# The first expert's weights: asked for later, laid out by column pieces, split one by one

## The chip, the cores and the metric

One core of one Trainium2 chip runs the whole program. The metric is device time in microseconds for one execution: the median of the runs of a kernel.

## The reference

Attention with a local window and block summaries is followed by a mixture-of-experts layer that sends every token to one expert. Cut to what matters:

```python
# q, k, v: [4 batches, 8 heads, 768 positions, 64]
scores = concat(mask(|i-j| < 16, q k^T / 8), q max32(k)^T / 8 + log 32)
x = softmax(scores) @ concat(v, mean32(v))          # -> [4, 768, 512], float32
logits = x @ w_gate                                  # [4, 768, 8 experts]
for b, s:                                            # a chain along s
    e = argmax(logits) if s == 0 or sigmoid(x @ w_local) < 0.5 else previous e
    h = max(x[b, s] @ w1[e], 0)                      # w1[e]: 512 x 1024
    out[b, s] = softmax(logits)[e] * (h @ w2[e])     # w2[e]: 1024 x 512
```

## The kernel before

**Attention.** 16 pairs of heads (4 batches, 4 pairs each) are worked through in 32 groups, two groups per pair. The main loop runs over G = 0 to 34, because it is a pipeline: iteration G makes the scores of group G (`s_mm`, L309 and L315), the maxima on VectorE (L321) and the exponentials on ScalarE (L325), transposes group G-2 (`t_stage`, L335, copied by ScalarE at L336), multiplies group G-3 with v (`a_mm`, L346) and normalises it into a tile `xs` (`a_norm`, L361 and L362). `a_mm` has one PSUM bank, which comes free when L362 has read it. There are three `xs` tiles for the eight that are written, and each is stored to `x_dram` by SyncE (L452, 876 KB) before it is written again. SyncE's queue also issues all loads, in program order; the last load of attention is `load_w(15)` (L182) in iteration 28.

**Beside attention.** When batch 0 is done, its routing (`route(0)`, then `early()`) runs on VectorE in small steps between the steps of attention. It finds the expert `e0` that takes most tokens of batch 0, and the rows of six blocks of 128 tokens, of which the first two are gathered from `x_dram`. `TIME` and `MORE` say how many of these small steps fit in each gap of an iteration, from iteration 28 on by the third entry of `TIME`.

**The first expert's weights.** w1 and w2 of `e0` come as eight chunks of 128 x 1024 float32 (512 KB): 0 to 3 are w1, 4 to 7 are w2. A chunk is fetched into one of four buffers `wst` (`wfetch`, L977, on SyncE) and then split into a high and a low part (`wsplit`): ScalarE copies the high part (L981), and the low part is a subtraction, on VectorE in one instruction (L984) or on GpSimd in four pieces of 256 columns (L989). `WBY` names the engine of each chunk. Chunk j of w1 holds the rows k = j of all 1024 columns. `WFETCH` and `WSPLIT` give the iterations in which chunks are fetched and chunks 0 to 3 split; a fetch of chunk 4 to 7 waits until the split of chunk 0 to 3 has left its buffer.

**The expert layer.** Blocks of 128 rows are worked through in pairs (`pair`). `tx` transposes a block of 128 gathered rows and splits it (L999, L1001). Layer 1 goes over four pieces of 256 columns of w1, each of two halves j with four k and three products (L1104 to L1106): 16 steps of six matmuls, and at the end of each piece ScalarE's ReLU (L1110) and VectorE's low part (L1112). Layer 2 (L1023 to L1025) takes eight slices of w2, twice. `START` puts the two `tx` and step 0 of layer 1 into iterations 33 and 34. After iteration 34, `last()` issues the other steps, splits w2's chunks after the steps given by `WLAST`, and between steps lets `flow` issue routing steps of batches 1 to 3 (`route(1)`, then `finish`), which run mostly on VectorE with a few small TensorE operations (L563 is the first). All engines work in program order.

Of the kernel before, what the change touches and what calls it, by code (L numbers as in the profile page):

```python
# [19 lines left out]
P = 128  # L20
# [11 lines left out]
E, DM, DF = 8, 512, 1024  # L32
KT, FT = DM // P, DF // P
# [13 lines left out]
OOB = 4096  # L47
WARM = 44

WFETCH = (25, 26, 26, 27, 28, 29, 30, 31)  # L50
WSPLIT = (28, 29, 30, 31)
WBY = "VGGVVGVG"

WLAST = (2, 5, 8, 11)
START = ((33, 1), (34, 0), (34, 1))
FIRST_L1 = 16

SPLIT_BY = ("VGVV", "VGVG")
# [2 lines left out]
PW1, PW2 = (0, 2, 4, 6), (10, 12, 14, 15)  # L61

ON_PE = {"PE": 2, "PE late": 4, "ACT": 4}
TIME, MORE = ((0.5, 0.2, 0.3), (0.7, 0.4, 0.3), (0.9, 0.5, 0.4)), 28

C_T, C_PE, C_WAIT, C_LONG, C_DVE, C_LAT, AHEAD = 0.65, 0.8, 0.3, 1.3, 0.14, 0.05, 1.5

# [3 lines left out]
class Kernel:  # L71
# [945 lines left out]
        self.split_ps(ps, h, l)  # L1017
        return h, l

    def mm(self, ps, ah, al, w, c0, first, last):  # L1020
        nc = self.nc
        wh, wl = self.hi[w][:, c0:c0 + 512], self.lo[w][:, c0:c0 + 512]
        nc.tensor.matmul(out=ps, lhsT=ah, rhs=wh, start=first, stop=False)  # L1023
        nc.tensor.matmul(out=ps, lhsT=ah, rhs=wl, start=False, stop=False)  # L1024
        nc.tensor.matmul(out=ps, lhsT=al, rhs=wh, start=False, stop=last)  # L1025
# [36 lines left out]
    def few(self, j):  # L1062

        nc, fw, b = self.nc, self.fw, j
        s1, s2 = self.raw
        ps = self.bank("s")[:, 0:DF // 4]
        for k in range(KT):
            for q in range(4):
                c0 = k * DF + DF // 4 * q
                nc.tensor.matmul(out=ps[FEW * q:FEW * q + FEW], lhsT=self.xf[b][:, k], rhs=s1[:, c0:c0 + DF // 4],  # L1070
                                 start=(k == 0), stop=(k == KT - 1))
        h = fw.tile([P, DF // 4], F32, name="fh")
        nc.scalar.activation(out=h, in_=ps, func=AF.Relu)
        yield
        ps = self.bank("t")[:, 0:DF // 4]
        for c in range(2):
            nc.tensor.transpose(out=ps[:, P * c:P * c + P], in_=h[:, P * c:P * c + P], identity=self.ident)
        hT = fw.tile([P, 2, 4, FEW], F32, name="fhT")
        nc.vector.tensor_copy(out=hT.rearrange("p c q t -> p (c q t)"), in_=ps)
        yield  # L1080
        ps = self.bank("a")[:, 0:P]
        for f in range(FT):
            for q in range(4):
                c0 = f * DM + P * q
                nc.tensor.matmul(out=ps[FEW * q:FEW * q + FEW], lhsT=hT[:, f % 2, f // 2], rhs=s2[:, c0:c0 + P],
                                 start=(f == 0), stop=(f == FT - 1))
        y = fw.tile([P, P], F32, name="fy")
        nc.vector.tensor_scalar(out=y, in0=ps, scalar1=self.p4[b], scalar2=None, op0=ALU.mult)
        nc.gpsimd.indirect_dma_start(out=self.out.rearrange("t (q d) -> (t q) d", q=4),
                                     out_offset=bass.IndirectOffsetOnAxis(ap=self.idx4[b], axis=0),  # L1090
                                     in_=y, in_offset=None, bounds_check=4 * T_ALL - 1, oob_is_err=False)

    def pair(self, i, mid, w1, w2):

        nc = self.nc
        xT, hT = self.xT, self.hT
        for f in range(0, FT, 2):
            ps = self.bank("s").rearrange("p (f t) -> p f t", f=2)
            for j in range(2):
                for k in range(KT):  # L1100
                    c0 = k * DF + P * (f + j)
                    xh, xl = [xT[:, k, part].rearrange("p h t -> p (h t)") for part in range(2)]
                    wh, wl = [w[0][:, c0:c0 + P] for w in (self.hi, self.lo)]
                    nc.tensor.matmul(out=ps[:, j], lhsT=wh, rhs=xh, start=(k == 0), stop=False)  # L1104
                    nc.tensor.matmul(out=ps[:, j], lhsT=wh, rhs=xl, start=False, stop=False)  # L1105
                    nc.tensor.matmul(out=ps[:, j], lhsT=wl, rhs=xh, start=False, stop=(k == KT - 1))  # L1106
                    if k % 2:
                        yield
            h, l = hT[:, f:f + 2, 0], hT[:, f:f + 2, 1]
            nc.scalar.activation(out=h, in_=ps, func=AF.Relu)  # L1110
            self.dve(0.6, self.t + 0.5)
            nc.vector.scalar_tensor_tensor(out=l, in0=ps, scalar=0.0, in1=h.bitcast(F32), op0=ALU.max, op1=ALU.subtract)  # L1112
        for half in range(2):
            yp = self.bank("a")
            s = slice(P * half, P * half + P)
            for f in range(FT):
                self.mm(yp, hT[:, f, 0, s], hT[:, f, 1, s], 1, f * DM, f == 0, f == FT - 1)
                yield
                j = FT * half + f
                pm = PM if i else PM0  # L1120
                if j in pm:
                    mid(pm.index(j))
                for at, w in (PW1, w1), (PW2, w2):
                    if j in at:
                        w(*(q for q in range(4) if at[q] == j))
            self.store(yp, 2 * i + half, 2 * i < EARLY)
        yield

    def single(self, i, mid, w1, w2):

        nc, fw = self.nc, self.fw
        hs = [fw.tile([P, 512], F32, name=f"hs{f}") for f in range(2)]

        def mm1(f, ks):
            for k in ks:
                if k == 0:
                    self.hp = self.bank("s")
                self.mm(self.hp, self.xT[:, k, 0, 0], self.xT[:, k, 1, 0], 0, k * DF + 512 * f, k == 0, k == KT - 1)
                if k == KT - 1:
                    nc.scalar.activation(out=hs[f], in_=self.hp, func=AF.Relu)  # L1140

        mm1(0, range(KT))
        mm1(1, (0, 1))
        hT = [self.th(hs[0], "h0"), None]
        mm1(1, (2, 3))
        w1(0, 1)
        yp = self.bank("a")

        def mm2(ks):
            for k in ks:  # L1150
                h, l = [x[:, P * (k % 4):P * (k % 4) + P] for x in hT[k // 4]]
                self.mm(yp, h, l, 1, k * DM, k == 0, k == FT - 1)

        mm2((0, 1))
        hT[1] = self.th(hs[1], "h1")
        mm2((2, 3))
        for h in range(2):
            mid(h)
        w1(2, 3)
        mm2(range(4, 8))  # L1160
        self.store(yp, i)
        w2(0, 1, 2, 3)

    def run(self):
        nc, tc = self.nc, self.tc
        CH = 1024
        NCH = KT * DF // CH
        jobs, st = {}, {}

        def at(G, point, f, *args):  # L1170
            jobs.setdefault((G, point), []).append((f, args))

        def wfetch(j):
            w, q = divmod(j, NCH)
            st["w", j] = self.awk.tile([P, CH], F32, name="wst", bufs=4)
            self.fetch(st["w", j], w, q * CH, (q + 1) * CH, st["e0"])

        def wsplit(j):
            w, q = divmod(j, NCH)
            self.split(w, q * CH, (q + 1) * CH, st.pop(("w", j)), nc.vector if WBY[j] == "V" else nc.gpsimd)  # L1180

        def have_e0():
            st["e0"] = nc.values_load(self.e0[0:1, 0:1], engines=(ENG.SP,), min_val=0, max_val=E - 1)
            for j in range(2 * NCH):
                if j < NCH:
                    at(WSPLIT[j], 1, wsplit, j)
                at(WFETCH[j], 1, wfetch, j)

        def have_rows(s0, s1):
            st["told"] = s1  # L1190
# [3 lines left out]
        def ask_rows():  # L1194
            st["rows"] = s1 = st["told"]
            while st["next"] < min(s1, st["free"]):
                self.gather(st["next"])
                st["next"] += 1
# [10 lines left out]
        def block0():  # L1209
            self.mw2 = self.pool("m_wk2")  # L1210
            self.xT = self.mw2.tile([P, KT, 2, 2, P], F32R, name="xT")
            self.hT = self.mw2.tile([P, FT, 2, 2 * P], F32R, name="hT")
            for i in range(2):
                while st["next"] <= i:
                    self.small(1, True)
                    ask_rows()
                self.tx(i, i)
                freed()
                yield

        def last():
            st["attention"] = False
            ask_rows()
            self.later(self.wait(), self.route(NS - 1), self.finish())
            for k in range(FIRST_L1):
                next(first)
                if k in WLAST:
                    wsplit(NCH + WLAST.index(k))
                self.flow(C_T)

        def reg(i, engines, hi):
# [54 lines left out]
        first = chain(block0(), self.pair(0, *calls(2)))  # L1286

        for G, i in START:
            at(G, i, lambda: next(first))
# [168 lines left out]
```

## Time and profile before

| | us |
|---|---|
| median of 3 runs | 444.74 (443.76 to 449.13) |
| the profiled execution, its own time | 444.76 |
| its span in the trace | 443.0 |
| TensorE busy in the span | 409.0 (92%) |
| mean granted TensorE clock | 0.987 of full speed |

The trace is one execution. Its times run from the start of the span, and 1.76 us of the execution's own time lie outside it. In the rows below, a time in square brackets is what the engine sat idle before an instruction, with what ended the wait. A name that ends in q (SPq) is an engine's sequencer.

### The profile page before, as it was taken

How to read it: one execution, taken by the hardware profiler on the slowest of the kernel's cores; microseconds unless marked ns; L12 is line 12 of the kernel's file. 1: busy time of each engine (PE TensorE's matmuls, PEld its weight loads, DVE VectorE, ACT ScalarE, POOL GpSimd, SP SyncE). 2: the span in 40 equal slices, each digit the busy share in tenths (PEclk: the TensorE clock that was granted, in tenths of full speed). 3: DMA queues.
4: the chain of work that ended last, by engine and by line, in shares of the span. 5: the costliest groups of instructions: out<-in, count | busy, mean ns of one | idle time of the engine just before them, and what ended most of it. 6: DMA issues, size and time to landing. Idle time of an engine off the chain costs nothing. (4 is left out here: it accounts for less than half of the span.)

```text
span 443.0 us, 11507 instructions
## 1 busy us (share of the span) xinstructions
PE 409.0 (92%) x4190; PEld 352.5 (80%) x4190; DVE 223.3 (50%) x455; ACT 182.9 (41%) x467; POOL 196.9 (44%) x288
## 2 busy tenths in 40 slices
PE   7799998898789999999999999999999999999950
PEld 6667786676579898989879788898978989898840
DVE  4678888886878775755212222137213621314510
ACT  3978887786853212165201111136206511115510
POOL 4397777687545201249311201209523820213940
PEclk9999999999999999999999999999999999999995
DMA  8999999999681208317979400304920950111770
GB/s 303 419 388 327 373 407 344 399 355 352 268 270 44 73 31 343 139 28 263 372 286 326 164 25 4 102 2 151 326 88 27 329 199 35 55 51 29 249 271 26
DMA packets 22853, 91.29 MB, mean 206 GB/s; under 512 B 2766, under 2 KB 3280, under 8 KB 19184
## 3 DMA queue, kind: packets, MB, share of 16 engines
q1 hardware_dynamic: 18176, 74.65, 45.3%
q0 software_dynamic: 4448, 15.42, 10.3%
q8 instruction: 40, 0.66, 0.6%
q14 instruction: 45, 0.37, 0.2%
q10 hardware_dynamic: 144, 0.20, 0.1%
HBM read 76.79 MB, written 13.60 MB: 204 GB/s over the span
## 5 line engine op out<-in xcount | busy, mean ns | idle before, releaser
L1104 PE MATMUL bs<-xT,h 128*128 128x256 f32 x352 | 100.7, 286 | 0.0
L1105 PE MATMUL bs<-xT,h 128*128 128x256 f32 x352 | 99.8, 283 | 0.5 <-DVE xT L1001 0.5
L1106 PE MATMUL bs<-xT,l 128*128 128x256 f32 x352 | 99.6, 283 | 0.0
L1110 ACT ACTIVATE hT<-bs 128x512 fp32r<-128x512 f32 x44 | 26.3, 598 | 117.5 <-PE bs L1106 113.2
L995 POOL DMA_INDIRECT xg<-x_dram,gidx x30 | 33.7, 1125 | 90.7 <-PE bt L1006 36.8
L1023 PE MATMUL ba<-h,hT 128*128 128x512 f32 x176 | 71.3, 405 | 0.3
L1025 PE MATMUL ba<-h,hT 128*128 128x512 f32 x176 | 68.9, 391 | 0.0
L1104 PEld LDWEIGHTS bs<-xT,h 128*128 128x128 f32 x352 | 67.4, 191 | 1.8 <-issue 1.2
L1024 PE MATMUL ba<-l,hT 128*128 128x512 f32 x176 | 68.7, 390 | 0.0
L1112 DVE SCALAR_TENSOR_TENSOR hT<-bs,hT 128x512 fp32r<-128x512 f32 x44 | 30.4, 691 | 75.5 <-ACT hT L1110 68.9
L1105 PEld LDWEIGHTS bs<-xT,h 128*128 128x128 f32 x352 | 67.4, 192 | 1.2 <-DVE xT L1001 0.7
L1106 PEld LDWEIGHTS bs<-xT,l 128*128 128x128 f32 x352 | 67.4, 192 | 0.2 <-DVE l L984 0.2
L1036 POOL DMA_INDIRECT out_dram<-yo,sidx x24 | 25.8, 1077 | 72.7 <-DVE yo L1035 25.3
L325 ACT ACTIVATE pr<-bs,nm 128x120 f32<-128x120 f32 x192 | 52.0, 377 | 8.2 <-DVE nm L321 7.9
L989 POOL TENSOR_TENSOR l<-stg,h 128x256 fp32r<-128x256 f32 x48 | 42.9, 924 | 7.4 <-ACT h L981 7.4
L261 POOL COPY vw<-vs 24x438 f32<-24x438 f32 x64 | 33.6, 564 | 23.3 <-ACT vs L251 10.0
L1025 PEld LDWEIGHTS ba<-h,hT 128*128 128x128 f32 x176 | 33.0, 188 | 7.4
L1023 PEld LDWEIGHTS ba<-h,hT 128*128 128x128 f32 x176 | 33.1, 188 | 6.9 <-ACTq L1258 0.6
L1024 PEld LDWEIGHTS ba<-l,hT 128*128 128x128 f32 x176 | 33.2, 189 | 5.7
L346 PE MATMUL ba<-vw,pt 121*64 121x74 f32 x768 | 32.1, 231 | 4.0 <-DMA wst<-in_w 1.7
L981 ACT CAST h<-stg 128x1024 fp32r<-128x1024 f32 x32 | 32.7, 1050 | 7.0 <-PE ba L1025 6.3
L346 PEld LDWEIGHTS ba<-vw,pt 121*64 121x64 f32 x768 | 27.3, 136 | 9.3 <-issue 6.3
(253 smaller groups left out, 623.0 us busy)
## 6 DMA issues: line engine op xcount, KB each, us to landing
stg<-in_w SPq DMA_DIRECT2D x20, 1024.0 KB, 6.1
vw<-in_vW SPq DMA_DIRECT2D x16, 888.0 KB, 7.6
raw<-in_w SPq DMA_DIRECT2D x8, 1024.0 KB, 11.8
x_dram<-xs SPq DMA_DIRECT2D x8, 876.0 KB
kp<-in_kT SPq DMA_DIRECT2D x16, 384.0 KB, 6.6
q<-in_qT SPq DMA_DIRECT2D x16, 384.0 KB, 6.4
vt<-in_vT SPq DMA_DIRECT2D x16, 384.0 KB, 9.0
wst<-in_w SPq DMA_DIRECT2D x8, 512.0 KB, 9.3
```

The costliest lines, as they stand in the source:

```text
L261: nc.gpsimd.tensor_copy(out=vf[n % 3][WL:W, t:t + NW // 4, 1:1 + PW], in_=vs.to_broadcast([NB, NW // 4, PW]))
L325: nc.scalar.activation(out=pr[:, h, u, :], in_=sp[:, h, u, :], func=AF.Exp, bias=nm[:, h, u:u + 1], scale=1.0)
L346: nc.tensor.matmul(out=ap[64 * c:64 * c + 64, u, h, :], lhsT=pt[0:W + 1, h, u, 64 * c:64 * c + 64], rhs=vw[n % 3][0:W + 1, 2 * (NG * g + u ...
L981: self.nc.scalar.copy(out=hi, in_=src)
L989: eng.tensor_tensor(out=lo[:, p], in0=src[:, p], in1=hi[:, p].bitcast(F32), op=ALU.subtract)
L995: self.nc.gpsimd.indirect_dma_start(out=t.rearrange("p a d -> p (a d)"), out_offset=None, in_=rows, in_offset=bass.IndirectOffsetOnAxis(ap ...
L1023: nc.tensor.matmul(out=ps, lhsT=ah, rhs=wh, start=first, stop=False)
L1024: nc.tensor.matmul(out=ps, lhsT=ah, rhs=wl, start=False, stop=False)
L1025: nc.tensor.matmul(out=ps, lhsT=al, rhs=wh, start=False, stop=last)
L1104: nc.tensor.matmul(out=ps[:, j], lhsT=wh, rhs=xh, start=(k == 0), stop=False)
L1105: nc.tensor.matmul(out=ps[:, j], lhsT=wh, rhs=xl, start=False, stop=False)
L1106: nc.tensor.matmul(out=ps[:, j], lhsT=wl, rhs=xh, start=False, stop=(k == KT - 1))
```

## The change

w1 is laid out in DRAM by pieces of 256 columns, so that chunk j of w1 is piece j of layer 1 with all four k. All readers of w1 address it accordingly. The four chunks of w1 are fetched in iteration 28, behind `load_w(15)`. Chunk 0 is split in iteration 32 and chunk 1 in iteration 34; the others are split in `last()`, after steps given by a longer `WLAST`. w2's chunks are fetched in `last()`: 4 and 5 at its start, behind the last two stores of `xs` on SyncE's queue; 6 and 7 behind the splits of chunks 2 and 3. The two `tx` and step 0 of layer 1 come half an iteration or one iteration earlier. GpSimd and VectorE take the low parts in turn, and the third entry of `TIME` is smaller.

```diff
-WFETCH = (25, 26, 26, 27, 28, 29, 30, 31)
-WSPLIT = (28, 29, 30, 31)
-WBY = "VGGVVGVG"
-WLAST = (2, 5, 8, 11)
-START = ((33, 1), (34, 0), (34, 1))
+WFETCH = 28
+WSPLIT = ((32, 1), (34, 0))
+WBY = "VGVGVGVG"
+WLAST = (1, 3, 6, 8, 10, 12)
+START = ((32, 1), (33, 0), (34, 0))
...
-TIME, MORE = ((0.5, 0.2, 0.3), (0.7, 0.4, 0.3), (0.9, 0.5, 0.4)), 28
+TIME, MORE = ((0.5, 0.2, 0.3), (0.7, 0.4, 0.3), (0.6, 0.3, 0.3)), 28
...
     def mm(self, ps, ah, al, w, cols, first, last):
-        wh, wl = self.hi[w][:, c0:c0 + 512], self.lo[w][:, c0:c0 + 512]
+        wh, wl = cols(self.hi[w]), cols(self.lo[w])
...
     def pair(...):
-                    c0 = k * DF + P * (f + j)
+                    c0 = 2 * P * (KT * (f // 2) + k) + P * j
...
     def have_e0():
-            for j in range(2 * NCH):
-                if j < NCH:
-                    at(WSPLIT[j], 1, wsplit, j)
-                at(WFETCH[j], 1, wfetch, j)
+            for j in range(NCH):
+                at(WFETCH, 1, wfetch, j)
+            for j, when in enumerate(WSPLIT):
+                at(*when, wsplit, j)
...
     def last():
             self.later(self.wait(), self.route(NS - 1), self.finish())
+            for j in range(NCH, NCH + len(WSPLIT)):
+                wfetch(j)
             for k in range(FIRST_L1):
                 next(first)
                 if k in WLAST:
-                    wsplit(NCH + WLAST.index(k))
+                    j = len(WSPLIT) + WLAST.index(k)
+                    wsplit(j)
+                    if j < NCH:
+                        wfetch(j + NCH)
                 self.flow(C_T)
...
-    w1 = inputs["moe_w1"].reshape(E, KT, P, DF).transpose(0, 2, 1, 3).reshape(E, P, KT * DF)
+    w1 = inputs["moe_w1"].reshape(E, KT, P, FT // 2, 2 * P).transpose(0, 2, 3, 1, 4).reshape(E, P, KT * DF)
```

In `at(G, point, ...)`, point 0 lies ahead of `a_mm` in iteration G and point 1 at its end.

## Rows read from the trace of the kernel before

**Rows 1.** The page: busy time by engine, and DMA's busy tenths in 40 slices.

```profile
PE 409.0 (92%) x4190; PEld 352.5 (80%) x4190; DVE 223.3 (50%) x455; ACT 182.9 (41%) x467; POOL 196.9 (44%) x288
DMA  8999999999681208317979400304920950111770
```

**Rows 2.** Busy time in stretches: stretch, length, five engines, PEclk, DMA share, GB/s.

```profile
98.00:106.00 8.00, 7.06 (x140) 5.41 (x132) 7.06 (x17) 5.82 (x25) 6.49 (x11) 1.00 0.96 321
105.47:127.60 22.13, 16.68 (x302) 13.07 (x298) 15.37 (x34) 16.63 (x51) 13.76 (x22) 1.00 0.76 280
128.00:134.00 6.00, 4.72 (x38) 4.54 (x39) 4.63 (x13) 1.94 (x3) 1.67 (x2) 1.00 1.01 370
135.00:425.00 290.00, 289.53 (x2002) 256.92 (x2001) 120.62 (x234) 82.66 (x117) 103.81 (x106) 1.00 0.41 146
```

**Rows 3.** Timeline of TensorE: start, duration, line, what, idle before.

```profile
110.26 1.00 PE L346 MATMUL ba<-vw,pt 121*64 121x74 f32 x24 [1.72 <-DMA wst<-in_w]
...
114.73 1.00 PE L346 MATMUL ba<-vw,pt 121*64 121x74 f32 x24 [1.46 <-DVE p L686]
...
122.53 0.54 PE L335 MATMUL bt<-ident,pr 128*120 128x128 f32 x3 [1.60 <-ACT vw L286]
...
128.45 0.39 PE L1105 MATMUL bs<-xT,h 128*128 128x256 f32 x1 [0.46 <-DVE xT L1001]
...
133.01 0.27 PE L563 MATMUL bt<-ident,val 128*18 128x128 f32 x1 [0.83 <-DVE val L560]
...
141.79 0.40 PE L1023 MATMUL ba<-h,hT 128*128 128x512 f32 x1
```

**Rows 4.** Timeline of VectorE in iterations 28 and 29.

```profile
109.39 0.62 DVE L362 TENSOR_TENSOR xs<-ba,dn 128x438 f32<-128x438 f32 x1 [3.31 <-DMA x_dram<-xs]
109.92 1.59 DVE L984 TENSOR_TENSOR l<-wst,h 128x1024 fp32r<-128x1024 f32 x1
...
111.53 0.86 DVE L321 TENSOR_REDUCE nm<-bs 128x6 f32<-128x720 f32 x1
```

**Rows 5.** Timeline of ScalarE: high parts (L981) and exponentials (L325), iterations 28 to 31.

```profile
106.84 1.03 ACT L981 CAST h<-wst 128x1024 fp32r<-128x1024 f32 x1
...
112.43 1.62 ACT L325 ACTIVATE pr<-bs,nm 128x120 f32<-128x120 f32 x6 [3.26 <-DVE nm L321]
113.90 1.08 ACT L981 CAST h<-wst 128x1024 fp32r<-128x1024 f32 x1
...
121.06 1.08 ACT L981 CAST h<-wst 128x1024 fp32r<-128x1024 f32 x1
```

**Rows 6.** Timeline of SyncE's queue: what was issued, and when.

```profile
92.92 0.69 SPq L977 DMA_DIRECT2D wst<-in_w  x1
...
98.39 0.39 SPq L452 DMA_DIRECT2D x_dram<-xs  x1
98.98 1.35 SPq L977 DMA_DIRECT2D wst<-in_w  x2
...
105.71 0.34 SPq L182 DMA_DIRECT2D vw<-in_vW  x1
...
111.53 12.37 SPq L977 DMA_DIRECT2D wst<-in_w  x4
126.64 4.06 SPq L452 DMA_DIRECT2D x_dram<-xs  x2
```

**Rows 7.** Everything on tile wst: durations in ns, min/median/max; landing times in us.

```profile
L989 POOL TENSOR_TENSOR l<-wst,h x16: 714/731/1392, 115.1 to 142.7; 128x256 fp32r<-128x256 f32 x16
...
L984 DVE TENSOR_TENSOR l<-wst,h x4: 1226/1296/1586, 109.9 to 137.0; 128x1024 fp32r<-128x1024 f32 x4
...
DMA to landing us min/median/max: 4.0/9.3/14.6
```

**Rows 8.** Timeline of GpSimd: the gather of block 6.

```profile
176.14 0.98 POOL L995 DMA_INDIRECT xg<-x_dram,gidx  x1 [1.81 <-issue]
```

**Rows 9.** Timeline of ScalarE: the first split of a later expert.

```profile
192.49 1.05 ACT L981 CAST h<-stg 128x1024 fp32r<-128x1024 f32 x1 [0.19 <-issue]
```

More of the change, by code (lines that the diff above doesn't have):

```diff
@@ L1018, in th, with mm @@
         return h, l
-    def mm(self, ps, ah, al, w, c0, first, last):
+    def mm(self, ps, ah, al, w, cols, first, last):
         nc = self.nc
-        wh, wl = self.hi[w][:, c0:c0 + 512], self.lo[w][:, c0:c0 + 512]
+        wh, wl = cols(self.hi[w]), cols(self.lo[w])
         nc.tensor.matmul(out=ps, lhsT=ah, rhs=wh, start=first, stop=False)
@@ L1068, in few @@
             for q in range(4):
-                c0 = k * DF + DF // 4 * q
+                c0 = 2 * P * (KT * q + k)
                 nc.tensor.matmul(out=ps[FEW * q:FEW * q + FEW], lhsT=self.xf[b][:, k], rhs=s1[:, c0:c0 + DF // 4],
@@ L1116, in pair @@
             for f in range(FT):
-                self.mm(yp, hT[:, f, 0, s], hT[:, f, 1, s], 1, f * DM, f == 0, f == FT - 1)
+                self.mm(yp, hT[:, f, 0, s], hT[:, f, 1, s], 1, lambda t: t[:, f * DM:f * DM + DM], f == 0, f == FT - 1)
                 yield
@@ L1137, in mm1 @@
                     self.hp = self.bank("s")
-                self.mm(self.hp, self.xT[:, k, 0, 0], self.xT[:, k, 1, 0], 0, k * DF + 512 * f, k == 0, k == KT - 1)
+                self.mm(self.hp.rearrange("p (a c) -> p a c", a=2), self.xT[:, k, 0, 0], self.xT[:, k, 1, 0], 0,
+                        lambda t: t.rearrange("p (a k c) -> p a k c", k=KT, c=2 * P)[:, 2 * f:2 * f + 2, k], k == 0, k == KT - 1)
                 if k == KT - 1:
@@ L1151, in mm2 @@
                 h, l = [x[:, P * (k % 4):P * (k % 4) + P] for x in hT[k // 4]]
-                self.mm(yp, h, l, 1, k * DM, k == 0, k == FT - 1)
+                self.mm(yp, h, l, 1, lambda t: t[:, k * DM:k * DM + DM], k == 0, k == FT - 1)
         mm2((0, 1))
```

## The prediction, made before the result

> **What bounds the kernel now.** I read the page first, then the stretches, and the timelines last. On the page TensorE is busy for 409.0 of 443.0 us, while the DMA engines are full for the first quarter of the span only [rows 1]. The stretches say where TensorE still has something to give: from 135 to 425 us it is busy for 289.53 of 290.00 us [rows 2]. From there on the time is TensorE's own work, which the change doesn't touch: the same products in the same number, at a granted clock that the row shows as 1.00. So the question is by how much earlier layer 1 begins, and whether it then runs through. A shift there moves the end by as much, if the routing behind it keeps up: the rows of block 6 are gathered at 176.14 us and the next expert's first split runs at 192.49 us, 16 us later, while TensorE never waits [rows 8, 9, 2]. That is room enough for VectorE to lag a few us behind.
>
> Iterations 29 to 34 lie between 105.47 and 127.60 us: 22.13 us, of which TensorE works 16.68, so 5.45 us are idle [rows 2]. The timeline names three of these gaps, 1.72, 1.46 and 1.60 us; then come 0.46 us at the start of layer 1 and 0.83 us within it, at the first routing operation [rows 3]. These sum up to 5.45 + 0.46 + 0.83 = 6.7 us, and no shift of layer 1 can be worth more.
>
> Behind the gaps stand the other two engines. VectorE sits for 3.31 us in front of `xs`, until a store of `x_dram` has landed; then come 1.59 us for the low part of chunk 0, and only then the maxima of group 29 [rows 4]. That store was asked for at 98.39 us and the tile is free at 109.39: 11 us in a queue that holds chunk 0, asked for at 92.92 us, ahead of it [rows 6, 4]. ScalarE waits 3.26 us for these maxima and then has no pause: three exponential groups with three copies of high parts between, some 1.08 us each [rows 5].
>
> **The change part by part.**
>
> *Fetches of w1 behind the last load.* Chunk 0 no longer lies ahead of the store. It has 524,288 bytes; at 321 GB/s (98 to 106 us) that is 1.6 us, at 370 (128 to 134 us) 1.4 [rows 2]. Chunks 1 and 2 were asked for 0.6 us behind the store [rows 6] and in a queue served in order would not delay it. If all three share the engines with it, 3 x 1.4 = 4.2 us go, more than the whole wait of 3.31. So the wait shrinks by something from 0 (if the store itself or the gathers beside it are what takes 11 us) to 3.31; I take 1.4, since chunk 0 alone is certainly ahead. SyncE has nothing behind the four fetches until the last stores, so they delay nobody. Chunk 0 lands late but in time: it is asked for at some 106 us [rows 6], and the longest landing seen, 14.6 us [rows 7], gives 120.6; with 1.03 and 1.30 us for the split that is 122.9, still ahead of step 0 at 124.5 (the sum below).
>
> *Split of chunk 0 out of iteration 28.* VectorE's 1.59 us in front of the maxima go [rows 4]. ScalarE's copy at 106.84 lay ahead of a wait [rows 5] and gives nothing.
>
> *Splits of chunks 1 to 3 out of iterations 29 to 31.* ScalarE had no pause there, so 3 x 1.08 = 3.24 us go [rows 5]. The smaller `TIME` takes some routing steps of about 0.2 us from VectorE as well; it has no wait of ScalarE behind it once the 1.59 us are gone, so I put it at 0.
>
> *Split of chunk 0 into iteration 32.* It stands between the two `tx`: its high part, 1.03 us, ahead of the last copies on ScalarE [rows 5], its low part, 1.30 us, ahead of the second `tx`'s low part on VectorE [rows 7]. Both lie on the way to step 0, so 2.33 us are given back. The range is 1.30 (if the copy fits into a pause) to 2.62 (with the longest low part, 1.59).
>
> *Chunks 1 to 3 in their turn.* Old layer 1 runs from 128.45 to 141.79 us, so one of its 16 steps takes 0.83 us [rows 3]. By the new layout steps 0 to 3 need chunk 0 alone. Chunk 1 is due after four steps, 3.3 us: 1.03 for the copy and 0.73 for the first of GpSimd's pieces [rows 5, 7]. Chunks 2 and 3 are split seven and nine steps ahead of their use. I cost them at nothing; what hides them is layer 1 itself, and without that cover each would cost about 1.8 us.
>
> *Fetches of w2 in `last()`.* They stand behind the last two stores of `xs`. The second store was asked for 0.38 us ahead of the end of the group of 4.06 us that begins at 126.64, at 130.32 us [rows 6]; some 4 us earlier that is 126.3. A fetch lands 4.0 us after the asking in an empty queue, 9.3 in the median [rows 7], so chunk 4 is there between 130.3 and 135.6. Its copy is written behind step 7, which ends at 128.45 - 3.9 + 8 x 0.83 = 131.2. So ScalarE and then VectorE stand for 0 to 4.4 us, with piece 1's ReLU and the routing steps queued behind them. TensorE needs chunk 4 and that ReLU only in layer 2, at 141.79 - 3.9 = 137.9, but the routing operations written into its queue wait for VectorE, as one did for 0.83 us [rows 3]. Bounds: -0.8 (that wait goes, since the order is another) and +4.4. I take +0.5, because the stretch from 128 to 134 us shows the two stores and the gathers cleared at 370 GB/s [rows 2], nearer to the short landing.
>
> **Sum.** 1.4 + 1.59 + 3.24 - 2.33 = 3.9 us earlier into layer 1; less 0.5 gives 3.4. Against the profiled execution's 444.76 us that is 441.36; it stands 0.02 us over the median, so I say 441.3.
>
> **The rivals.**
>
> *The store's wait stays.* Then the 1.4 us fall away: 442.8. For it: the queue was full before 92 us too [rows 1]. Against it: half a MB less has to pass.
>
> *All the idle time goes.* 444.76 - 6.7 = 438.0. It needs the store's whole wait to vanish and both splits in iteration 32 to fit beside other work. For it: three chunks moved, not one; against it: the 2.33 us stand in program order on the same two engines.
>
> *w2 comes late, and the kernel is slower.* The mechanism is ScalarE standing at chunk 4. It decides from the point where TensorE loses more than the 3.9 us won, and at 4.4 us of standing passed on in full it is 444.76 - 3.9 + 4.4 = 445.3. With the longest landing, 14.6 us [rows 7], chunk 4 is there at 140.9 and split at 143.2, 5.3 us after layer 2 wants it, and VectorE's standing of 9.7 us can reach TensorE through routing operations: 446.2 to 450.6, centre 448. For it: before, w2 was asked for from 111.53 us on, in attention [rows 6]; now nothing is ahead of need. Against it: the median of 9.3 us was measured in a stretch with a full queue.
>
> The Trainium skill (Trainium Kernel Development and Optimization, Best Practices) says to double-buffer so that DMA overlaps compute, which speaks for asking early and so against this change; by that rule the result would be the rival just told. The trace speaks against applying it here before 106 us, where the DMA share is 0.96 in the stretch from 98 to 106 us and an early fetch pushes something else back [rows 2].
>
> *Low parts on two engines at once slow each other.* A piece on GpSimd takes 731 ns in the median and 1392 at most, one on VectorE 1226 to 1586 [rows 7]. With VectorE and GpSimd in turn at six splits within twelve steps, they meet more often. If the last chunk's four pieces all take 1392 ns, it is ready 2.6 us later; passed on in full that gives 441.3 + 2.6 = 443.9.
>
> The Trainium skill (SBUF — State Buffer, Who interferes with whom) says that a VectorE instruction with two SBUF inputs contends with a GpSimd instruction that reads SBUF, as both low parts are. The spread of 714 to 1392 ns fits that [rows 7].
>
> **How the numbers follow.** Forecast (439.5 to 442.3): 0.50. The store's wait stays: 0.12. All idle time goes: 0.12. Low parts collide: 0.12. w2 late and slower: 0.14. The range runs from 438.0 less the 0.3 us by which one execution may differ, 437.7, to 445.3, the near end of the slow rival; what is left out is most of that rival, about 0.12, and some 0.04 below. Two per cent is 8.9 us, about what a measurement of this kernel can tell from no change. Faster by over 2% would be under 435.8, more than all the idle time: 0.02. Slower by over 2% is over 453.6 and needs more than the longest landing: 0.02. Within: 0.96.
>
> **What would show each step.** In the changed trace VectorE's wait before `xs` in iteration 28 should be about 1.9 us or gone, no L984 or L981 should stand before iteration 32, and ScalarE's exponentials of groups 29 to 31 should follow each other 3 us apart. The first uninterrupted L1105 should come at about 124.5 us, the first L1023 of layer 2 at about 138.4, and TensorE should be without a gap of 1 us between. If the fetches of chunk 4 land after 131 us, ScalarE's wait before L981 will name a DMA; then look whether L563 and its followers on TensorE wait for VectorE. The prediction is wrong if layer 1 begins as early as said but has gaps of more than 2 us, if something other than these two engines holds iterations 29 to 31 at their old pace, or if TensorE begins to wait behind 170 us for routing results that the earlier start has overtaken.

## The result, and the profile after

The changed kernel takes 448.40 us in the median of 20 runs (444.47 to 453.38), the kernel before 445.52 in 20 runs beside them. The ratio is 1.0086, with a 95% interval from 1.0059 to 1.0112: 0.9% slower, inside the 2% of no change, but outside the forecast range of 437.7 to 445.3 and on the other side of before. The ratio leaves out the runs that lie over 1.5% above the fastest one of their kernel, so it isn't the quotient of the two medians. The profiled execution took 448.24 us, with a span of 446.5 us.

The page of the changed kernel: busy time by engine, then the granted clock and DMA's busy tenths in 40 slices.

```profile
PE 412.5 (92%) x4190; PEld 355.6 (80%) x4190; DVE 221.6 (50%) x455; ACT 183.3 (41%) x467; POOL 195.3 (44%) x288
...
PEclk9999999998998999999999999999999999999995
DMA  8999999989574114706987500204930850210770
```

The number of matmuls is the same as in [rows 1], yet TensorE is busy for 3.5 us longer: a part of its work ran slower. The granted clock has an 8 in two of the first thirteen slices, of 11.2 us each; the second is the slice from 134 us on. DMA's tenths are 5, 7, 4 from 112 us on, where before had 6, 8, 1: w2's chunks, which the kernel before asks for in attention, now come in layer 1.

The stretches of the changed kernel, with the columns of [rows 2]: the one in which the kernel before had iterations 29 to 34, a piece of layer 1, and the rest.

```profile
105.47:127.60 22.13, 20.22 (x352) 15.91 (x352) 15.18 (x38) 17.79 (x57) 9.83 (x18) 0.99 0.62 220
...
140.00:143.00 3.00, 3.00 (x16) 3.00 (x16) 1.72 (x3) 1.00 (x2) 3.00 (x4) 0.50 0.03 5
135.00:425.00 290.00, 287.14 (x1980) 254.94 (x1979) 120.56 (x234) 83.41 (x118) 103.83 (x107) 0.99 0.42 148
```

Ahead of layer 1 the change did its work: of 22.13 us TensorE now works 20.22, against 16.68 in [rows 2]. (The stretch is the same by the clock and not by the work: here group 28 begins at 105.44 us and layer 1 at 126.50.) But in the stretch from 135 us on, in which TensorE was never to wait by the prediction, 2.86 us are idle instead of 0.47, and from 140 to 143 us the granted clock is 0.50, that is 1.2 GHz. TensorE's timeline shows both.

TensorE of the changed kernel, from iteration 27 to layer 2 (start, duration, line, what, idle before).

```profile
100.98 0.63 PE L315 MATMUL bs<-kb,q 64*64 64x120 f32 x13 [2.03 <-issue]
...
123.84 0.54 PE L335 MATMUL bt<-ident,pr 128*120 128x128 f32 x3 [0.93 <-DVE xT L1001]
...
126.50 0.38 PE L1105 MATMUL bs<-xT,h 128*128 128x256 f32 x1 [0.16 <-DVE xT L1001]
...
127.29 1.00 PE L346 MATMUL ba<-vw,pt 121*64 121x74 f32 x24
...
134.62 0.27 PE L563 MATMUL bt<-ident,val 128*18 128x128 f32 x1 [0.39 <-DVE val L560]
...
139.25 0.23 PE L569 MATMUL bt<-ident,pm 18*128 18x18 f32 x1 [2.22 <-DVE pm L566]
...
139.90 0.41 PE L1104 MATMUL bs<-xT,h 128*128 128x256 f32 x1
140.11 0.41 PE L1105 MATMUL bs<-xT,h 128*128 128x256 f32 x1
...
144.10 0.40 PE L1023 MATMUL ba<-h,hT 128*128 128x512 f32 x1
...
146.00 0.18 PE L596 MATMUL bt<-sc,cb 128*128 128x8 bf16 x1 [0.35 <-DVE sc L592]
```

Layer 1 begins at 126.50 us instead of 128.45 [rows 3], and the three gaps of [rows 3] ahead of it are gone. Layer 2 begins at 144.10 instead of 141.79. In between TensorE waits for 2.22 us ahead of L569, a routing operation, and the 15 layer-1 matmuls behind it, from 139.90 to 143.10, follow each other 0.21 us apart instead of 0.12, which costs 3.20 - 15 x 0.12 = 1.4 us. Behind the first L1105 stands L346, the product with v of group 31: it used to lie ahead of layer 1 and now lies in it.

What L569 waited for is to be read from three engines' rows: first SyncE's requests, then ScalarE, then VectorE.

SyncE of the changed kernel (its second number is the time that it took to issue the group).

```profile
109.26 2.21 SPq L977 DMA_DIRECT2D wst<-in_w  x4
...
127.22 2.36 SPq L452 DMA_DIRECT2D x_dram<-xs  x2
129.85 5.66 SPq L977 DMA_DIRECT2D wst<-in_w  x4
```

ScalarE of the changed kernel: exponentials of groups 29 to 31, the high part of chunk 0, the high part of chunk 4, and the ReLU behind it.

```profile
112.11 1.63 ACT L325 ACTIVATE pr<-bs,nm 128x120 f32<-128x120 f32 x6
...
115.04 1.63 ACT L325 ACTIVATE pr<-bs,nm 128x120 f32<-128x120 f32 x6
...
119.08 1.63 ACT L325 ACTIVATE pr<-bs,nm 128x120 f32<-128x120 f32 x6
...
122.96 1.05 ACT L981 CAST h<-wst 128x1024 fp32r<-128x1024 f32 x1
...
135.97 1.05 ACT L981 CAST h<-wst 128x1024 fp32r<-128x1024 f32 x1 [3.71 <-DMA wst<-in_w]
136.93 0.59 ACT L1110 ACTIVATE hT<-bs 128x512 fp32r<-128x512 f32 x1
```

VectorE of the changed kernel: `xs` in iteration 28, then the low part of chunk 4 and what stands behind it.

```profile
108.82 0.61 DVE L362 TENSOR_TENSOR xs<-ba,dn 128x438 f32<-128x438 f32 x1
...
137.06 1.23 DVE L984 TENSOR_TENSOR l<-wst,h 128x1024 fp32r<-128x1024 f32 x1 [2.58 <-ACT h L981]
138.20 0.68 DVE L1112 SCALAR_TENSOR_TENSOR hT<-bs,hT 128x512 fp32r<-128x512 f32 x1
138.80 0.40 DVE L566 TENSOR_TENSOR_SCAN pm<-bt,zero 18x128 f32<-18x128 f32 x1
```

Read upwards from L569: it wants `pm`, which L566 writes at 138.80; L566 needs nothing of chunk 4, but stands behind L984 and L1112 in VectorE's program order; L984 waits for ScalarE's copy, L1112 for ScalarE's ReLU, and ScalarE stood for 3.71 us in front of chunk 4, asked for at 129.85 behind the two stores and landed 6.1 us later. TensorE needs chunk 4 itself only at 144 us.

### The profile page after: what moved, and what is told of

Read it like the earlier page. It is cut to its first block, busy times and chain, and to the rows that moved or that the text cites. A ratio compares the mean times of both kernels' runs of the same rounds, so it can differ in the third digit from the quotient of the medians.

```text
span 446.5 us, 11514 instructions
## 1 busy us (share of the span) xinstructions
PE 412.5 (92%) x4190; PEld 355.6 (80%) x4190; DVE 221.6 (50%) x455; ACT 183.3 (41%) x467; POOL 195.3 (44%) x288
## 5 line engine op out<-in xcount | busy, mean ns | idle before, releaser
L1104 PE MATMUL bs<-xT,h 128*128 128x256 f32 x352 | 101.4, 288 | 0.0
L1105 PE MATMUL bs<-xT,h 128*128 128x256 f32 x352 | 100.5, 285 | 0.2 <-DVE xT L1001 0.2
L1023 PE MATMUL ba<-h,hT 128*128 128x512 f32 x176 | 71.4, 406 | 0.3
L1104 PEld LDWEIGHTS bs<-xT,h 128*128 128x128 f32 x352 | 68.1, 193 | 1.8 <-issue 1.2
L1105 PEld LDWEIGHTS bs<-xT,h 128*128 128x128 f32 x352 | 68.2, 194 | 1.0 <-DVE xT L1001 0.6
L1025 PE MATMUL ba<-h,hT 128*128 128x512 f32 x176 | 68.9, 391 | 0.0
L1112 DVE SCALAR_TENSOR_TENSOR hT<-bs,hT 128x512 fp32r<-128x512 f32 x44 | 30.4, 690 | 71.9 <-ACT hT L1110 62.8
L1036 POOL DMA_INDIRECT out_dram<-yo,sidx x24 | 24.9, 1036 | 72.2 <-DVE yo L1035 25.3
L325 ACT ACTIVATE pr<-bs,nm 128x120 f32<-128x120 f32 x192 | 52.0, 381 | 5.8 <-DVE nm L321 5.6
L261 POOL COPY vw<-vs 24x438 f32<-24x438 f32 x64 | 32.5, 548 | 30.9 <-issue 14.8
L1025 PEld LDWEIGHTS ba<-h,hT 128*128 128x128 f32 x176 | 33.0, 188 | 7.3
L1023 PEld LDWEIGHTS ba<-h,hT 128*128 128x128 f32 x176 | 33.1, 188 | 6.8 <-ACTq L1264 0.6
L981 ACT CAST h<-stg 128x1024 fp32r<-128x1024 f32 x32 | 32.7, 1050 | 7.0 <-PE ba L1025 6.3
L346 PE MATMUL ba<-vw,pt 121*64 121x74 f32 x768 | 32.6, 235 | 0.9 <-POOL vw L261 0.7
L984 DVE TENSOR_TENSOR l<-stg,h 128x1024 fp32r<-128x1024 f32 x20 | 27.4, 1380 | 12.1 <-ACT h L981 10.5
```

Source lines behind the costliest of these rows:

```text
L261: nc.gpsimd.tensor_copy(out=vf[n % 3][WL:W, t:t + NW // 4, 1:1 + PW], in_=vs.to_broadcast([NB, NW // 4, PW]))
L325: nc.scalar.activation(out=pr[:, h, u, :], in_=sp[:, h, u, :], func=AF.Exp, bias=nm[:, h, u:u + 1], scale=1.0)
L346: nc.tensor.matmul(out=ap[64 * c:64 * c + 64, u, h, :], lhsT=pt[0:W + 1, h, u, 64 * c:64 * c + 64], rhs=vw[n % 3][0:W + 1, 2 * (NG * g + u ...
L981: self.nc.scalar.copy(out=hi, in_=src)
```

## The experiments

Three theories were to be told apart. **A**: w2 comes late, and its splits block the queues of ScalarE and VectorE until a routing operation stops TensorE. **B**: the loss arises ahead of layer 1, in the 2.03 us hole at L315 in iteration 27 or at the store in iteration 28. **C**: low parts on GpSimd and VectorE slow each other and the routing steps. The kernels of one comparison ran on one chip. Besides the times I compare three lengths in each profile: from the first matmul of group 27 (L309) to the first uninterrupted L1105; from there to the first L1023 (layer 1); from there to the first L1105 of the next pair of blocks (layer 2). From that point to the last L1025 it is 272.5 to 272.9 us in 13 of the 18 profiles, those of before and of the changed kernel among them. What follows takes 16.0 and 16.3 us in the two profiles of before and 14.4 to 17.0 in four of the changed kernel, so what makes the changed kernel slower lies ahead. In the five others it is 274.3 to 276.4; the last section tells what these have.

**w2 asked for ahead of need.** When attention's buffers for q, k and v are given back in iteration 32, SBUF has room for two more buffers; chunks 4 and 5 go there and are asked for in iteration 32, 6 and 7 into the buffers of chunks 0 and 1 as these come free.

```diff
-                    self.free_banks()
+                    self.free_banks(); self.awk2 = ctx.enter_context(tc.tile_pool(name="a_wk2", bufs=1, side="right"))
...
+            at(32, 0, wfetch, NCH)
+            at(32, 0, wfetch, NCH + 1)
...
+            at(*WSPLIT[0], wfetch, NCH + 2)
...
-            for j in range(NCH, NCH + len(WSPLIT)):
-                wfetch(j)
+            wfetch(NCH + 3)
...
-                    if j < NCH:
-                        wfetch(j + NCH)
```

> The changed kernel with w2's chunks 4 and 5 in two buffers of their own, asked for in iteration 32, chunk 6 behind the split of chunk 0, chunk 7 at the start of the last stage. Theory A (w2 comes late: ScalarE stood 3.71 us at chunk 4, VectorE 2.58 us behind it, and TensorE 2.22 us at L569 behind VectorE, after which 15 matmuls ran at the lower clock, 0.21 us apart instead of 0.12): ScalarE's wait at L981 and the gap at L569 go, no matmul of layer 1 runs at 0.21 us, and the time falls from 448.4 by 2.2 + 1.4 = 3.6 to about 444.8, just under before. Theory B (the 2.03 us hole in iteration 27 and the slow matmuls behind it are the loss, and come with the changed program): the gap at L569 may go, but iteration 27 keeps its hole, and the time stays over 446.5. Theory C (low parts on VectorE and GpSimd collide): pieces on GpSimd stay as long as 1.7 us and layer 2 still waits for them.

**The same late w2, split later.** Only the place of w2's splits in the engines' program order changes.

```diff
-WLAST = (1, 3, 6, 8, 10, 12)
+WLAST = (1, 3, 10, 12, 13, 14)
```

> The changed kernel with the splits of w2's chunks written behind steps 11, 13, 14 and 15 of layer 1 instead of 7, 9, 11 and 13; fetches as they are. Theory A: the ReLU and the routing scan come ahead of the late chunk, so the gap at L569 goes; what is left is a wait of up to 2 us at the start of layer 2 or within it, and the time falls by 1.5 to 3 us to 445.5 to 447. If only the arrival of the data counts, and not what is queued behind it, the whole wait moves into layer 2 and the time stays at 448.4. Theory B: no change, 448.

**Only chunk 4 ahead of the stores**, asked for behind the split of chunk 0, in whose buffer it goes.

```diff
+            at(*WSPLIT[0], wfetch, NCH)
...
-            for j in range(NCH, NCH + len(WSPLIT)):
+            for j in range(NCH + 1, NCH + len(WSPLIT)):
```

> The changed kernel with only chunk 4's fetch moved: right behind the split of chunk 0 in iteration 32, so ahead of the last two stores on SyncE's queue. Asked for at about 125.3 instead of 129.85, it lands by 131.5, when its copy is due at 132. Theory A: ScalarE's 3.71 us at chunk 4 shrink to under 1, but chunks 5 to 7 still come behind the stores, at 133.5 and later; the gap at L569 shrinks under 1 us and the time falls by about 3 us to 445.5. Theory B: 448.

**The kernel before, with the two stores of batch 2 asked for one iteration earlier**, so that the one which `xs` waits for in iteration 28 lies ahead of chunk 0 on SyncE's queue.

```diff
-                    stores.append((G + LA + (0 if b == B - 1 else 1), t, x))
+                    stores.append((G + LA + (0 if b >= B - 2 else 1), t, x))
```

> The kernel before with one edit: the two stores of batch 2 are issued one iteration earlier, the first of them ahead of the first chunk of w1. The wait of 3.31 us in front of xs in iteration 28 goes. If that wait was on the path, TensorE's gap of 1.72 us goes too and the time falls by 1.7 to 3.3 us to 442.2 to 443.8; if ScalarE's three copies of high parts hold iterations 29 to 31 anyway, it falls by under 1 us.

Measured, as ratios to before: w2 ahead 1.0001 (0.9962 to 1.0041), split later 1.0001 (0.9964 to 1.0039), chunk 4 first 1.0022 (0.9990 to 1.0054), store earlier 0.9990 (0.9953 to 1.0026). None differs from before by the times alone; the profiles say more. With the later splits, ScalarE still waits for chunk 4, and TensorE does not.

ScalarE, VectorE and TensorE of the kernel with later splits:

```profile
131.04 0.60 ACT L1110 ACTIVATE hT<-bs 128x512 fp32r<-128x512 f32 x1 [1.28 <-PE bs L1106]
133.52 1.05 ACT L981 CAST h<-wst 128x1024 fp32r<-128x1024 f32 x1 [1.88 <-DMA wst<-in_w]
```

```profile
132.49 0.40 DVE L566 TENSOR_TENSOR_SCAN pm<-bt,zero 18x128 f32<-18x128 f32 x1
...
134.60 1.23 DVE L984 TENSOR_TENSOR l<-wst,h 128x1024 fp32r<-128x1024 f32 x1 [0.41 <-ACT h L981]
```

```profile
132.12 0.27 PE L563 MATMUL bt<-ident,val 128*18 128x128 f32 x1 [0.40 <-DVE val L560]
...
133.74 0.23 PE L569 MATMUL bt<-ident,pm 18*128 18x18 f32 x1
...
137.81 0.40 PE L1023 MATMUL ba<-h,hT 128*128 128x512 f32 x1
```

The requests stand where they stood, and ScalarE waits 1.88 us, but L566 is ahead of L984, L569 has no wait, and layer 1 lasts 13.81 us instead of 17.60. So late data alone cost layer 1 nothing: the time was lost because a routing step stood behind the split that waited for them. With w2 ahead there is no DMA wait at all, and layer 1 lasts as long, 13.82 us:

SyncE and ScalarE of the kernel with w2 ahead; the seven fetches are w1 and chunks 4 to 6.

```profile
107.44 18.03 SPq L977 DMA_DIRECT2D wst<-in_w  x7
127.49 1.93 SPq L452 DMA_DIRECT2D x_dram<-xs  x2
129.68 1.04 SPq L977 DMA_DIRECT2D wst<-in_w  x1
```

```profile
131.05 1.99 ACT L981 CAST h<-wst 128x1024 fp32r<-128x1024 f32 x2
```

Chunk 4 alone ahead of the stores was asked for at 126.24 us. ScalarE doesn't wait for it any more and L569 has no gap, as theory A expected; the wait moves on to chunk 5, which is still asked for behind the stores, at 130.84 us.

ScalarE and TensorE of the kernel with chunk 4 first; the first row is the high parts of chunks 3 and 4, the second that of chunk 5.

```profile
132.15 1.99 ACT L981 CAST h<-wst 128x1024 fp32r<-128x1024 f32 x2
...
137.41 1.05 ACT L981 CAST h<-wst 128x1024 fp32r<-128x1024 f32 x1 [2.33 <-DMA wst<-in_w]
```

```profile
137.92 0.23 PE L569 MATMUL bt<-ident,pm 18*128 18x18 f32 x1
```

Behind this wait TensorE stands for 0.70 us at L575, the next routing operation, and layer 1 lasts 14.79 us. With the earlier store the kernel before has no wait at `xs` any more, but L335 waits 2.16 us for ScalarE's copy L286 where it waited 1.60 [rows 3], and the time stays: behind the store stood ScalarE.

**The changed kernel and the kernel before again**, without edits, beside two combinations. The first is w2 ahead with later splits, `WLAST = (1, 3, 8, 10, 12, 13)`; the second is w2 ahead with w1 asked for when before asks for it:

```diff
-WFETCH = 28
+WFETCH = (25, 26, 26, 27)
...
-                at(WFETCH, 1, wfetch, j)
+                at(WFETCH[j], 1, wfetch, j)
```

> The changed kernel once more, for a second profile. Theory A (w2 late) says that the wait of ScalarE at chunk 4 (3.71 us), the gap at L569 (2.22) and the span from the scores of group 28 to the first L1105 of the second pair (51.5 us, before 51.3) come again, within 1 us. Theory B (the hole in iteration 27 is the changed program's own) says that the hole of 2.03 us at L315 with slow matmuls behind it comes again; the three other variants, which have the same program up to there, showed 0.93, 1.47 and 1.49 us, so I expect 0.9 to 1.5.

> The kernel before once more, for a second profile: how far one execution differs from the next. From the scores of group 28 to the first L1105 of the second pair 51.3 us, within 1 us, with the store's wait of about 3.3 us and the three gaps of TensorE; the start of group 28 may differ by 1.5 us from 102.54.

> The run with w2 asked for ahead, and its splits behind steps 9, 11, 13 and 14 of layer 1. If each of these two takes away the same wait (ScalarE and VectorE standing ahead of the routing scan), together they give no more than the later one alone: the stretch from the scores of group 28 to the second pair is 48.5 us, and the time 443 to 445. If they take away different waits, it is under 48 us.

> The run with w2 asked for ahead, but w1's chunks asked for in iterations 25 to 27 as in the kernel before; their splits stay where the change puts them. If asking behind the last load is what took the 3.31 us wait in front of xs away, the wait is back (1.5 to 3.3 us) and iterations 28 to 31 take 12 us instead of 10.9; time up by 1 to 3 us from 444.2. If the wait had its length from something else, nothing changes.

Measured: changed again 447.42 us, 1.0029 (0.9999 to 1.0060); w2 ahead and late splits 444.03, 0.9936 (0.9907 to 0.9966); w1 early 444.31, 0.9944 (0.9906 to 0.9982). In the changed kernel's second profile L569 waits 2.45 us, and layer 1 lasts 17.87. With w1 early the store's wait is back, as was expected, but the time isn't up.

VectorE with w2 ahead and w1 early: `xs` in iteration 28.

```profile
109.95 0.62 DVE L362 TENSOR_TENSOR xs<-ba,dn 128x438 f32<-128x438 f32 x1 [3.50 <-DMA x_dram<-xs]
```

The second profile of before speaks against B, which is shown first by VectorE (`xs` in iteration 28), then by TensorE (L315 in iteration 27). The last row is that L315 in the first profile.

```profile
109.10 0.62 DVE L362 TENSOR_TENSOR xs<-ba,dn 128x438 f32<-128x438 f32 x1 [0.22 <-DMA x_dram<-xs]
```

```profile
100.85 0.63 PE L315 MATMUL bs<-kb,q 64*64 64x120 f32 x13 [2.58 <-issue]
```

```profile
99.50 0.63 PE L315 MATMUL bs<-kb,q 64*64 64x120 f32 x13 [0.94 <-issue]
```

Here the hole in iteration 27 is 2.58 us and the wait for the store 0.22; in the first profile it is 0.94 and 3.31 [rows 4]. The two replace each other: a store that was asked for ahead of the hole lands during it. In the 17 profiles whose store was not moved, the six with a hole of 2.0 us or more have a wait of at most 0.54 us at `xs`, the eleven others 1.4 to 3.7. The sum of hole and wait is 4.25 and 2.80 us in before (mean 3.5) and 2.03, 3.11, 3.04 and 5.12 in four profiles of the changed kernel (mean 3.3).

**w2 later still; low parts on VectorE; first `tx` later; the best with w1 early.** The first is the changed kernel with the fetches of chunks 4 and 5 written behind step 2 of layer 1 instead of ahead of step 1. The second is w2 ahead with `WBY = "VGVGVVVV"`. The third is w2 ahead, late splits and `START = ((33, 0), (33, 1), (34, 0))`. The fourth is w2 ahead, late splits and `WFETCH = (25, 26, 26, 27)`.

> The changed kernel with the fetches of chunks 4 and 5 moved behind step 2 of layer 1 in program order; on SyncE's queue that is behind nothing new, because chunk 6 came next there anyway. So it is a test of the order on the queue alone: theory A expects the same asking times within 0.3 us, ScalarE's wait of 3.7 to 4.0 us at chunk 4, the gap of 2.2 to 2.4 us at L569 and the time of the changed kernel, 447.4 to 448.4. If the gap depended on where the fetches stand in the program and not on when SyncE comes to them, it would move.

> The run with w2 asked for ahead, and the low parts of chunks 5 and 7 on VectorE instead of GpSimd. Theory C (GpSimd's subtractions slow VectorE's small routing steps: L581 to L592 took 0.43 to 0.86 us there, 0.18 to 0.46 in the kernel before) expects these steps back at 0.18 to 0.46 us, the wait of 1.0 us at L596 gone and layer 2 (first L1023 to the next pair's L1105) at 12.0 to 12.5 us instead of 13.5. If the wait comes from VectorE's own load, two more low parts of 1.2 us make it longer by up to 2.4 us.

> The best run so far (w2 asked for ahead, its splits later) with the first tx half an iteration later. All kernels with the change show 0.9 us of TensorE waiting at L335 for VectorE to read the first tx's bank. If that wait is the order's doing it goes, and the first L1105 comes 0.5 to 0.9 us earlier after the scores of group 31 (11.1 to 11.7 us so far), time down by under 1 us. If the two splits and two tx just form one chain on ScalarE and VectorE, nothing changes.

> The best run so far, but w1's chunks asked for in iterations 25 to 27 as before the change. If asking behind the last load is worth what the prediction gave it, 1.4 us and up to 3.3, this is slower than the best run by that much, with the wait in front of xs back. If the hole in TensorE's instructions in iteration 27 or 31 just takes the place of that wait, both are the same within 1 us.

Measured: 0.9991 (0.9957 to 1.0025), 0.9968 (0.9934 to 1.0001), 1.0025 (0.9991 to 1.0058) and 0.9940 (0.9905 to 0.9974). The first edit moved nothing in the trace: SyncE asks at 129.61 us, since the two stores ahead of the fetches set that time, and L569 waits 2.29 us. By its requests and waits it is the changed kernel once more, and its layer 1 lasts 16.17 us, because here no stretch of low clock follows the gap. But its time, expected at 447.4 to 448.4 us, is 445.64, that of before; why stays open. The second shows C at work on VectorE's small routing steps.

VectorE with w2 ahead, beside GpSimd's pieces (L581 and L592 are routing steps), and then the same steps with the pieces on VectorE:

```profile
139.78 0.43 DVE L581 TENSOR_TENSOR ev<-vm,carx 128x18 int32<-128x18 f32 x1
...
141.77 0.86 DVE L592 TENSOR_TENSOR_SCAN sc<-c,oh 128x144 bf16<-128x144 f32 x1
```

```profile
145.58 0.18 DVE L581 TENSOR_TENSOR ev<-vm,carx 128x18 int32<-128x18 f32 x1
...
146.35 0.46 DVE L592 TENSOR_TENSOR_SCAN sc<-c,oh 128x144 bf16<-128x144 f32 x1
```

The steps take about twice as long beside GpSimd, TensorE waits 1.0 us for L592 at L596, and layer 2 lasts 13.47 instead of 12.95 us: in these profiles C is real, and worth some 0.5 us; the times (0.9968 beside 1.0001) don't tell the two apart. A later first `tx` has no wait at L335, but 0.8 us at L1104, 1.0 at L1105 and 1.1 at L596 in its place, and a granted clock of 0.51 from 131 to 134 us; its 1.0025 stands against 0.9936 for the kernel that it was made from, so it is slower.

**Four side by side:** the changed kernel, its late splits, the best one (w2 ahead, late splits, w1 early), and the best with the low part of chunk 7 on VectorE too (`WBY = "VGVGVGVV"`; it is chunk 7 that moves, where the expectation names the chunks otherwise).

> The changed kernel once more, on the same chip as the next three. The gap of 2.2 to 2.4 us at L569 comes again. If the lower clock behind it is as much of the loss as the gap, this profile shows matmuls 0.21 us apart for 3 us behind the gap (as in two of three so far) and the stretch from the scores of group 27 to the second pair is 58 us; without the low clock 56.6 us. Time 1.003 to 1.006 of before.

> The changed kernel with w2's splits later, data as late as in the changed kernel. Theory A: the gap at L569 is gone, no lower clock in layer 1, and it is faster than the changed kernel of the same call by 2.2 us and up to 3.7: 0.994 to 0.999 of before. If the late data itself is the loss, both are the same.

> w2 asked for ahead, its splits later, w1's chunks asked for in iterations 25 to 27 as before the change: 0.994 of before again, 3 us faster than the changed kernel, with the fetch of w1 behind the last load worth nothing.

> The same with the low part of chunk 6 on GpSimd as it is and that of chunk 7 on VectorE. Theory C (GpSimd's pieces slow VectorE's routing steps): layer 2 gets shorter by up to 0.5 us, time 0.993. If VectorE's own load counts, longer by up to 1.2 us, time 0.996.

Measured: 448.02 us, 1.0051 (1.0021 to 1.0081); 444.88, 0.9978 (0.9945 to 1.0011); 443.59, 0.9953 (0.9919 to 0.9988); 444.11, 0.9956 (0.9916 to 0.9997). The later splits alone take 3.1 us off the changed kernel, the best version 4.4, and chunk 7 on VectorE changes nothing that shows. The changed kernel's third repeat has the whole chain again.

ScalarE and TensorE of that repeat, and a stretch behind the gap (columns of [rows 2]):

```profile
139.53 1.05 ACT L981 CAST h<-wst 128x1024 fp32r<-128x1024 f32 x1 [3.77 <-DMA wst<-in_w]
```

```profile
142.80 0.23 PE L569 MATMUL bt<-ident,pm 18*128 18x18 f32 x1 [2.27 <-DVE pm L566]
```

```profile
142.00:146.00 4.00, 3.20 (x26) 3.17 (x27) 3.23 (x8) 2.49 (x4) 3.92 (x5) 1.00 0.19 73
```

The lengths in the profiles, in us:

| kernel | group 27 to L1105 | layer 1 | layer 2 | sum |
|---|---|---|---|---|
| before, two profiles | 30.63, 31.26 | 13.34, 13.27 | 12.03, 12.03 | 56.0, 56.6 |
| changed, three profiles | 28.29, 27.40, 29.34 | 17.60, 17.87, 16.16 | 12.82, 12.61, 13.16 | 58.7, 57.9, 58.7 |
| w2 later still | 27.22 | 16.17 | 13.20 | 56.6 |
| late splits, two profiles | 27.02, 27.21 | 13.81, 13.82 | 13.02, 13.33 | 53.9, 54.4 |
| chunk 4 first | 27.33 | 14.79 | 13.56 | 55.7 |
| w2 ahead | 27.33 | 13.82 | 13.47 | 54.6 |
| w2 ahead, low parts on VectorE | 27.70 | 13.28 | 12.95 | 53.9 |
| w2 ahead, w1 early | 30.48 | 13.84 | 13.49 | 57.8 |
| w2 ahead, late splits | 28.33 | 13.81 | 12.50 | 54.6 |
| the same, first `tx` later | 28.98 | 16.20 | 12.03 | 57.2 |
| w2 ahead, late splits, w1 early (best), two profiles | 27.03, 27.87 | 13.83, 13.81 | 12.50, 12.51 | 53.4, 54.2 |
| best, chunk 7 on VectorE | 29.78 | 13.82 | 12.36 | 56.0 |
| before, stores earlier | 30.39 | 13.45 | 12.04 | 55.9 |

## Why the prediction was wrong

The step that failed is **"Fetches of w2 in `last()`", +0.5 us out of bounds from -0.8 to +4.4**. The prediction named the chain (ScalarE and VectorE stand, the routing steps queue behind them, a routing operation holds TensorE) and gave its rival a chance of 0.14, but took the short landing, because the queue looked cleared at 370 GB/s. Chunk 4 landed 6.1 us after its asking at 129.85 us, so ScalarE stood for 3.71 us, and by the time this reached TensorE it was 2.22, at L569. In four profiles of this program (w2 later still counted as one) it is 2.22 to 2.45 us. Without it layer 1 lasts 13.8 us, with it 16.2 to 17.9: the term is +2.3 to +4.1. The upper end holds what the prediction had no term for, a stretch of low clock behind the gap. Undoing it in two ways that share nothing, earlier data or a later split, brings the same 13.8 us: that much is shown.

Three sizes in this step were off together. The fetch was forecast 1.8 us behind layer 1's start (126.3 against 124.5) and came 3.35 behind it (129.85 against 126.50): the last `xs`, its store and the fetches behind it on SyncE's queue wait for L346 of group 31, which now stands behind step 0. ScalarE reached the copy 5.8 us behind that start, at 132.26, instead of 6.7. And the queue was not clear: the DMA share is 1.01 from 129.85 to 136 us, as it was in the row of 370 GB/s [rows 2]. The landing times of [rows 7] were a poor guide besides. The trace of before gives a landing for only two of its eight fetches, 4.05 and 14.62 us, and 9.3 is the middle between them.

This term alone doesn't make the miss; at its upper end the prediction's sum would still be 445.0 us. By the lengths, 3.4 us less than before's 56.3 were forecast, and the changed kernel takes 1.7 more, 58.0 in the mean of four. Of these 5.1 us the fetches of w2 make 2.2 (layer 1 is 3.6 us longer than before in the mean, 0.9 of it group 31's product, and 0.5 were forecast), the stretch ahead of layer 1 makes 1.0 (2.9 us shorter and not 3.9), and group 31's product and layer 2, which had no term in the sum, 0.9 each.

The rival was priced with the longest landing, by layer 2's need of chunk 4 and by a stand of VectorE of up to 9.7 us that reaches TensorE through routing operations. Chunk 4 was split in time for layer 2. The time went by the second path, with a stand of 2.58 us, at a scan of 0.40 us that doesn't read w2 at all. That the rival's centre, 448, is about the median measured is luck: other losses, which it didn't count, make up the rest.

**Chunk 0 ahead of the store, 1.4 us:** half right for the wait, not shown in the time. With a hole under 1.5 us in iteration 27 the wait at `xs` is 2.75 to 3.50 us in the three profiles that ask for w1 early and have the store where before has it, and 1.38 to 2.42 in seven of the eight that ask late (3.65 in the eighth); about 1.9 was forecast. With a longer hole there is next to no wait either way. Hole and wait make 3.5 us together before and 3.3 after, and asking for w1 as early as before costs the best version nothing in its time (0.9940 beside 0.9936). The wait of 3.31 us in the one profile of before was an execution with a short hole.

**Splits out of iterations 28 to 31, into 32:** about right. 1.59 + 3.24 - 2.33 = 2.5 us were forecast; group 27 to L1105 lasts 30.9 us in the mean before and 28.1 in the mean of the changed kernel's four profiles, 2.9 shorter, in which the term of chunk 0 is contained; with w1 early it is 28.8 in the mean of four profiles, 2.2 shorter. The low part in iteration 32 is on the way, as said; the prediction didn't foresee that L335 would wait 0.93 us there, for the bank that the first `tx` holds.

**Layer 1's start as a milestone:** overlooked that step 0 now stands ahead of L346 of group 31, 24 products of 0.9 us together, which then fall into layer 1. Of the 2.9 us some 2.0 are gained. The prediction's lower bound for L563, -0.8, was half met: its wait went from 0.83 [rows 3] to 0.39.

**Chunks 1 to 3 in their turn, and everything behind 170 us:** right. No wait for w1 shows in layer 1, and from the second pair on the length is that of before.

**Low parts that meet:** forecast as a rival of up to 2.6 us. Layer 2 of the first pair lasts 0.6 to 1.2 us longer than before in the changed kernel and 0.5 with the best version. The edit of the low parts shows a share of GpSimd's pieces of about 0.5 in it; the rest I did not take apart.

By these lengths the changed kernel loses 1.7 us. By the ratios it lost 3.8, 1.3 and 2.3 us in three comparisons, and w2 later still, which counts as its fourth profile, lost nothing (0.9991). That difference stays open: group 27 itself began between 96.98 and 101.19 us in the profiles, with the same instructions ahead of iteration 25, and two or three profiles of a kernel don't tell that from chance. For the same reason the late splits, 2.1 us shorter than before by the lengths, are only 0 to 1.0 us faster by the ratios. What the times do show is the comparison side by side, 448.02 us beside 444.88 with nothing but the splits moved.

## What to carry to other kernels

Before a load is moved later, find the first instruction that waits for it in program order, not its first use, and list what stands behind that instruction on its engine, then on the engines that wait for those. A copy that may wait belongs behind everything short that another engine needs soon; here that order was worth 3.1 us with the data as late as ever. And one profile's wait at a store or load is a poor price, as is a median of two landings: see how many values stand behind it, and take a second profile of the same kernel before a term of the sum rests on it.

## What the runs showed of the hardware

In all profiles there is a hole at the same L315 of iteration 27, 0.9 to 2.9 us long, in which TensorE waits for nothing that the trace names ("issue"), while the DMA share from 97 to 105 us is 0.79 to 1.00. Smaller ones, of 0.5 to 1.9 us, stand at L315 of iterations 29 and 31 in eleven of the fifteen profiles with the change and in none of the three without it; in three of the changed kernel's four they make 1.6 to 2.4 us together. Another shows in five of the eight profiles of kernels with w2 ahead and in none of the ten others: 1.6 to 2.7 us ahead of an L1023 at some 420 us, which makes these five longer there. In the second profile of the best version, TensorE's timeline has it so:

```profile
417.13 0.39 PE L1023 MATMUL bs<-h,xT 128*128 128x512 f32 x1 [1.59 <-issue]
```

The same program's first profile has no such row. What TensorE waits for in these holes, and why the last one goes with this group of kernels, stays open.

TensorE's granted clock fell to 0.50 (1.2 GHz) from 140 to 143 us behind the gap of 2.22 us at L569 in the changed kernel, and to 0.66 in the mean of 141.5 to 145 us behind the gap of 2.45 in its second profile; behind gaps of 2.29 and 2.27 us in the two others it stayed at 1.00. Behind the hole in iteration 27 it was 0.55 from 102 to 105 us in the changed kernel (2.03 us of hole) and 0.73 from 100.85 to 103.85 us in the second profile of before (2.58), but 1.00 in the first (0.94). So the low clock behind that hole is not the changed program's own. Behind the five holes at some 420 us it stayed at 1.00. Such a gap can cost more than its own length (1.4 us more at L569), and it doesn't do so each time.
